# Query, key and value loads one pair earlier, and the shared chunk's tanh ahead of a pair's exponentials

## The chip, the cores and the metric

The kernel runs on one core of one Trainium2 chip. The metric is the device time of one execution, in microseconds (us).

## The reference, cut to what matters

```python
def _attn_ref(q, k, v, cap):                       # q, k, v: 2 x 12 x 448 x 64
    scores = (1.0 / np.sqrt(64)) * np.matmul(q, k.transpose(0, 1, 3, 2))
    scores = cap * np.tanh(scores / cap)
    scores = scores - np.max(scores, axis=-1, keepdims=True)
    attn = np.exp(scores)
    attn = attn / (np.sum(attn, axis=-1, keepdims=True) + 1e-09)
    return np.matmul(attn, v).astype(np.float32)
...
    x = np.ascontiguousarray(attn_out.transpose(0, 2, 1, 3)).reshape(B * S, H * D)   # 896 x 768
    x = _moe_ref(x=x, **moe_kwargs)      # x @ w_in, h * sigmoid(1.702 h), @ w_out
    return _moe2_ref(x=x, **moe2_kwargs) # rms norm, silu(x @ w_gate) * (x @ w_val), @ w_out
```

Everything is float32.

## The kernel before, in words

The program has two parts. `attention()` (lines 193 to 508) works on 12 pairs of heads (`NPR`); `rest()` (line 510 on) does the two feed-forward layers, with TensorE as its main engine. A scheduler does not reorder anything: every engine and every DMA queue runs its instructions in the order in which the Python code issues them. All loads and stores named here go to SyncE's queue (SPq in the profile).

A pair's k and q arrive as float32 in a tile `kq` and are split by VectorE into a high and a low part (`split_kq`, a cast in line 253 and a subtraction in line 254), so that three products give the accuracy. A head's 448 keys are three chunks of 128 and a rest of 64; the two heads' rests share a fourth chunk, the shared chunk (`NC`).

The loop of line 442 has 13 passes. Pass p, for 0 < p < 12, issues per engine:

- SyncE: `load_kq(p + 2)` (lines 217, 218: k 256 KB, q 224 KB), `load_v(p + 1)` (line 224, 256 KB), in the first three passes a weight tile `raw` (line 112, 768 KB), `spread(p - 3)` (line 367, which reads back the reciprocals of an earlier pair from DRAM), and late in the pass `keep_recips(p - 1)` (line 362, which stores the reciprocals of pair p-1 to DRAM and so waits for line 357).
- TensorE: score products of chunks 1 and 2 of pair p and chunk 0 of pair p+1 (`scores`, line 272, six products each), the shared chunk's (`scores_last`, line 280, three), the outputs of pair p-1 (`outputs`, line 318, 32 products), the sums of its exponentials (`sums`, line 352, 16).
- ScalarE: tanh of the three chunks (line 299), the exponential of chunks 0 and 1 (`exp(pa[p])`, line 302), a decode step if `plan_a` has one, the shared chunk's tanh (`tanh(p, NC)`, line 299), the exponential of the rest (`exp(pb[p])`).
- VectorE: `norm(p - 5)` from pass 5 on (lines 386, 398, 405), `split_kq(p + 2)`, `add_two(p)` (line 336, adds the two halves of `pa`), decode steps if `plan_d` has any, `copy_out(p - 1)` (line 330), the reciprocal of the sums of pair p-1 (line 357).
- GpSimd: `add_third(p)` (line 340, adds a part of `pb` to the tile of `add_two`).

The decode steps unpack the first weight tiles, whose words hold floats: on ScalarE `size` (line 127), `high_part` (line 174); on VectorE `clip` (131), `field` (135), `top` (159), `low` (165), `low_part` (179). In passes 1 to 6 `plan_a` and `plan_d` (lines 427 to 434) put them between the others; `clip` of a tile needs its `size`, `low_part` its `high_part`.

Buffers make further waits. `kq` has two, `v` three. The pool `ps_v` has two PSUM buffers, taken in turn by `scores_last(p)`, `outputs(p - 1)`, `sums(p - 1)`, `scores_last(p + 1)` and so on: `scores_last(p + 1)` waits for `copy_out(p - 1)`, `outputs(p)` for the reciprocal of pair p-1, `sums(p - 1)` for `tanh(p, NC)`. Of the scores' three buffers, each is free again after its tanh.

Of the kernel before, what the change touches and what calls it, by code (L numbers as in the profile page):

```python
# [8 lines left out]
F32 = mybir.dt.float32  # L9
# [8 lines left out]
def attn_moe_kernel(  # L18
# [15 lines left out]
    B, D = 2, 64  # L34
# [8 lines left out]
    NC = 3  # L43
# [63 lines left out]
    def load_to(u):  # L107
        while nload[0] <= min(u, len(units) - 1):
            w = nload[0]
            t = pools['raw'].tile([128, 6, 128, 2], U32, tag="raw", name="raw")  # L110
            for b0, n, s in units[w]:
                nc.sync.dma_start(out=t[:, b0:b0 + n].rearrange("p k f t -> p k (f t)"), in_=s)
            raw_t[w] = t
            nload[0] += 1
# [66 lines left out]
    def run(op, w):  # L181
        if w < len(units) and (op, w) not in done:
            done.add((op, w))
            op(w)
# [8 lines left out]
    def attention():  # L193
        with ExitStack() as actx:
            ap_ = actx.enter_context(tc.tile_pool(name="at", bufs=2, reuse_waits="tile"))
# [5 lines left out]
            XW = KW + S  # L201
# [9 lines left out]
            xs, raws, vs, pa, pb, zt, nr, ts_ = {}, {}, {}, {}, {}, {}, {}, {}  # L211

            def load_kq(p):
                if p >= NPR:
                    return
                t = raws[p] = ap_.tile([128, XW], F32, tag="kq", name="kq")
                nc.sync.dma_start(out=t[:, 0:KW], in_=k[p])
                nc.sync.dma_start(out=t[:, KW:XW], in_=q[p])

            def load_v(p):  # L220
                if p >= NPR:
                    return
                vs[p] = ap_.tile([128, 2 * (NC + 1), D], F32, tag="v", name="v", bufs=3)
                nc.sync.dma_start(out=vs[p].rearrange("p c d -> p (c d)"), in_=v[p])

            cuts = [slice(KW, XW), slice(0, 128), slice(128, KW)]
# [22 lines left out]
            def split_kq(p):  # L249
                t = raws.pop(p)  # L250
                x = ap_.tile([128, 2, XW], F32R, tag="x", name="x", bufs=3)
                xs[p] = [(x[:, a, KW:XW], (x[:, a, 0:KW],)) for a in range(2)]
                nc.vector.tensor_copy(x[:, 0], t)  # L253
                nc.vector.tensor_tensor(out=x[:, 1], in0=t, in1=f(x[:, 0]), op=ALU.subtract)
# [11 lines left out]
            def scores(p, c):  # L266
                if p >= NPR:
                    return
                ps = sc[p, c] = ps_s.tile([128, 2, 512], F32, tag="s", name="s")
                for n, (a, m) in enumerate(TERMS):  # L270
                    for e in range(2):
                        nc.tensor.matmul(
                            out=ps[:, e, 0:S], lhsT=keys(p, a, c)[half[e]],
                            rhs=xs[p][m][0][half[e]], start=(n == 0), stop=(n == 2),
                        )

            def scores_last(p):
                ps = sc[p, NC] = ps_v.tile([128, 512], F32, tag="v", name="v")
                for n, (a, m) in enumerate(TERMS):
                    nc.tensor.matmul(  # L280
                        out=ps[:, 0:S], lhsT=keys(p, a, NC), rhs=xs[p][m][0], start=(n == 0), stop=(n == 2)
                    )

            def tanh(p, c):
                if p >= NPR:
                    return
                if c == 0:
                    pa[p] = ap_.tile([128, 2, 2, S], F32, tag="pa", name="pa", bufs=3)
                if c == 2:
                    pb[p] = ap_.tile([128, 3, S], F32, tag="pb", name="pb", bufs=3)  # L290
                if c < 2:
                    t = pa[p][:, c]
                elif c == 2:
                    t = pb[p][:, 0:2]
                else:
                    t = pb[p][:, 2]
                src_ = sc.pop((p, c))
                src_ = src_[:, 0:S] if c == NC else src_[:, :, 0:S]
                nc.scalar.activation(out=t, in_=src_, func=AF.Tanh, scale=tsc)  # L299

            def exp(t):
                nc.scalar.activation(out=t, in_=t, func=AF.Exp, scale=capt)  # L302
# [7 lines left out]
            def outputs(p, cs=range(NC + 1)):  # L310
                if 0 in cs:
                    opened[p] = ps_v.tile([128, 512], F32, tag="v", name="v")
                ps = opened[p]
                for c in cs:
                    for n in range(4):
                        e, d0 = n // 2, n % 2 * 32
                        w = vs[p][:, e * NC + c if c < NC else 2 * NC + e]
                        nc.tensor.matmul(  # L318
                            out=ps[32 * n:32 * n + 32, 0:S], lhsT=w[:, d0:d0 + 32],
                            rhs=probs(p, c)[:, e] if c < NC else pb[p][:, 2],  # L320
                            start=(c == 0), stop=(c == NC), skip_group_check=True,
                        )
# [41 lines left out]
            def spread(p):  # L364
                d = nr[p].rearrange("(e j) n -> e (j n)", j=2)
                nr[p] = zrp.tile([128, S], F32, tag="r", name="r", bufs=3)
                nc.sync.dma_start(out=nr[p], in_=d.unsqueeze(1).to_broadcast([2, 64, S]))
# [41 lines left out]
            def norm(p):  # L409
                for step in (norm_mul, norm_hi, norm_lo):  # L410
                    step(p)
# [7 lines left out]
            constants()  # L419
            load_kq(1)  # L420
            load_v(0)

            warm = ps_v.tile([128, 512], F32, tag="v", name="v")
            for _ in range(WARM):
                nc.tensor.matmul(out=warm[:, 0:S], lhsT=ones, rhs=xA[0][:, 0, 0:S], start=True, stop=True)

            plan_a = {
                1: [(size, 0)], 2: [(size, 1)], 3: [(high_part, 0)], 5: [(high_part, 1)],
                12: [(square, 2), (sign, 2), (mask, 2)],
            }  # L430
# [5 lines left out]
            def decode(plan, p):  # L436
                for op in plan.get(p, ()):
                    run(*op)

            split_first(ts, x)  # L440

            for p in range(NPR + 1):
                load_kq(p + 2)
                load_v(p + 1)
                if p < 3:
                    load_to(p)
                if p == 0:
                    scores(0, 0)
                    tanh(0, 0)
                    exp(pa[0][:, 0])  # L450
                    scores(0, 1)
                    tanh(0, 1)
                    exp(pa[0][:, 1])
                    scores(0, 2)
                    tanh(0, 2)
                    scores_last(0)
                    tanh(0, NC)
                    exp(pb[0])
                    outputs(0, (0,))
                    split_kq(1)  # L460
                    scores(1, 0)
                    outputs(0, (1,))
                elif p < NPR:
                    tanh(p, 0)
                    scores(p, 1)
                    tanh(p, 1)
                    scores(p, 2)
                    tanh(p, 2)
                    exp(pa[p])
                    decode(plan_a, p)  # L470
                    scores(p + 1, 0)
                    scores_last(p)
                    tanh(p, NC)
                    exp(pb[p])
                else:
                    decode(plan_a, p)
                if 3 <= p < NPR:
                    spread(p - 3)
                if 5 <= p < NPR - 2:
                    norm(p - 5)  # L480
                if p + 2 < NPR:
                    split_kq(p + 2)
                if p < NPR:
                    add_two(p)
                decode(plan_d, p)
                if p == 1:
                    outputs(0, (2, NC))
                elif p:
                    outputs(p - 1)
                if NPR - 1 <= p:  # L490
                    spread_late(p - 2)
                if p:
                    if p < NPR:
                        copy_out(p - 1, "D")
                    sums(p - 1)
                    if p < NPR - 2:
                        keep_recips(p - 1)
                if p < NPR:
                    add_third(p)
                if NPR - 3 <= p < NPR:  # L500
                    norm(p - 4)
                if p == NPR:
                    copy_out(p - 1, "A")
                    some = (p - 3, p - 2, p - 4)
                    for step in (norm_mul, norm_hi, norm_lo):
                        for q_ in some:
                            step(q_)
# [340 lines left out]
    with tc.manual_schedule():  # L848
        tail = attention()
        rest(*tail)  # L850
# [64 lines left out]
```

## Time and profile before

| | |
|---|---|
| Runs | 623.2, 625.25, 626.21 us; median 625.25 us |
| Profiled execution | 623.85 us, its span 622.1 us |
| TensorE (PE) busy | 591.3 us, 95% of the span, mean granted clock 0.988 |
| VectorE (DVE) busy | 454.4 us, 73% |
| ScalarE (ACT) busy | 389.4 us, 63% |
| GpSimd (POOL) busy | 65.8 us, 11% |
| DMA | 67.91 MB, mean 109 GB/s |

A line of a timeline gives the start, the duration, the engine and line, the operation with the tile that it writes and the one it reads, a count, and in brackets how long the engine was idle before it and what ended that. PE is TensorE's products, PEld its weight loads. PEclk is the granted share of TensorE's full clock of 2.4 GHz, so 0.50 is 1.2 GHz. The duration shown reaches to where the result has left the engine; the next instruction may start a little sooner.

### The profile page before, as it was taken

How to read it: one execution, taken by the hardware profiler on the slowest of the kernel's cores; microseconds unless marked ns; L12 is line 12 of the kernel's file. 1: busy time of each engine (PE TensorE's matmuls, PEld its weight loads, DVE VectorE, ACT ScalarE, POOL GpSimd, SP SyncE). 2: the span in 40 equal slices, each digit the busy share in tenths (PEclk: the TensorE clock that was granted, in tenths of full speed). 3: DMA queues.
4: the chain of work that ended last, by engine and by line, in shares of the span. 5: the costliest groups of instructions: out<-in, count | busy, mean ns of one | idle time of the engine just before them, and what ended most of it. 6: DMA issues, size and time to landing. Idle time of an engine off the chain costs nothing.

```text
span 622.1 us, 8470 instructions
## 1 busy us (share of the span) xinstructions
PE 591.3 (95%) x3385; PEld 499.4 (80%) x3385; DVE 454.4 (73%) x553; ACT 389.4 (63%) x507; POOL 65.8 (11%) x51
## 2 busy tenths in 40 slices
PE   7857887899999999999999999999999999999997
PEld 4423333389989888888988989999988899999997
DVE  5676678779866644666778899998388887688842
ACT  6956668679975554777866774766456674356400
POOL 0221222100000000000012201210022200022100
PEclk9987999999999999999999999999999999999999
DMA  8332532116335241333333332334123343332012
GB/s 277 102 115 72 163 122 84 44 53 200 119 129 155 83 125 55 122 128 103 103 102 101 106 126 91 136 102 153 52 101 103 102 152 104 100 103 102 0 72 106
DMA packets 54449, 67.91 MB, mean 109 GB/s; under 512 B 2918, under 2 KB 49162, under 8 KB 54410
## 3 DMA queue, kind: packets, MB, share of 16 engines
q1 hardware_dynamic: 54122, 67.15, 33.4%
q8 instruction: 26, 0.43, 0.3%
q10 hardware_dynamic: 288, 0.23, 0.1%
q14 instruction: 13, 0.11, 0.1%
HBM read 64.59 MB, written 2.78 MB: 108 GB/s over the span
## 4 chain that ended last, share of the span: by engine, by line
PE 82%; DVE 8%; DMA 4%; ACT 2%; issue 2%; SPq 1%; DVEq 0%
PE b L568 22%; PE b L567 22%; PE b L566 22%; PE b L776 14%; DMA kq<-in_q 4%; DVE rs L357 2%; DVE ts L336 2%; PE v L318 2%; DVE x L253 1%; DVE z L330 1%; DMA first<-in_k 1%; ACT pa L302 1%; ACT pa L299 1%; DVE dec L159 1%; DVE dec L165 1%
## 5 line engine op out<-in xcount | busy, mean ns | idle before, releaser
L566 PE MATMUL b<-x,ring 128*128 128x512 f32 (+1 forms) x480 | 174.0, 362 | 2.2 <-DVE z L389 2.2
L568 PE MATMUL b<-x,ring 128*128 128x512 f32 (+1 forms) x480 | 174.3, 363 | 0.0
L567 PE MATMUL b<-x,ring 128*128 128x512 f32 (+1 forms) x480 | 174.1, 363 | 0.0
L566 PEld LDWEIGHTS b<-x,ring 128*128 128x128 f32 x480 | 90.1, 188 | 12.7 <-DVE z L389 2.6
L567 PEld LDWEIGHTS b<-x,ring 128*128 128x128 f32 x480 | 90.1, 188 | 9.9
L568 PEld LDWEIGHTS b<-x,ring 128*128 128x128 f32 x480 | 90.1, 188 | 9.4
L776 PE MATMUL b<-ring,uA 128*128 128x384 f32 x504 | 87.8, 334 | 0.0
L776 PEld LDWEIGHTS b<-ring,uA 128*128 128x128 f32 x504 | 87.4, 188 | 0.0
L153 DVE SCALAR_TENSOR_TENSOR dec<-raw,dec 128x768 uint32<-128x768 uint32 x66 | 67.8, 1028 | 24.7 <-ACT dec L149 23.4
L159 DVE SCALAR_TENSOR_TENSOR dec<-raw,dec 128x768 uint32<-128x768 uint32 x68 | 75.1, 1104 | 1.1
L179 DVE TENSOR_TENSOR ring<-dec,ring 128x768 fp32r<-128x768 f32 x68 | 66.8, 984 | 4.5 <-ACT ring L174 4.5
L568 PE MATMUL b<-g,ring 128*128 128x384 f32 (+1 forms) x192 | 70.0, 365 | 0.0
L567 PE MATMUL b<-g,ring 128*128 128x384 f32 (+1 forms) x192 | 69.9, 364 | 0.0
L566 PE MATMUL b<-g,ring 128*128 128x384 f32 (+1 forms) x192 | 69.6, 362 | 0.0
L165 DVE SCALAR_TENSOR_TENSOR dec<-raw,dec 128x768 uint32<-128x768 uint32 x68 | 66.7, 981 | 1.5
L174 ACT ACTIVATE ring<-dec 128x768 fp32r<-128x768 f32 x68 | 56.7, 834 | 17.4 <-DVE dec L165 8.7
L145 ACT ACTIVATE dec<-dec,edge 128x768 f32<-128x768 f32 x66 | 61.5, 932 | 1.0
L141 ACT ACTIVATE dec<-raw 128x768 f32<-128x768 f32 x66 | 59.1, 896 | 0.5 <-DVE ring L179 0.5
L149 ACT ACTIVATE dec<-dec 128x768 f32<-128x768 f32 x66 | 55.6, 843 | 1.5
L744 POOL TENSOR_TENSOR a<-a,gg 128x512 f32<-128x512 f32 (+1 forms) x18 | 29.3, 1628 | 188.9 <-DVE gg L737 188.9
L747 ACT ACTIVATE uA<-a 128x512 fp32r<-128x512 f32 (+1 forms) x24 | 13.9, 578 | 46.3 <-POOL a L744 34.5
L598 DVE TENSOR_TENSOR g<-gg,g 128x384 fp32r<-128x384 f32 (+1 forms) x32 | 20.0, 626 | 27.4 <-ACT g L595 27.2
(92 smaller groups left out, 648.2 us busy)
## 6 DMA issues: line engine op xcount, KB each, us to landing
raw<-in_moe_w_out SPq DMA_DIRECT2D x20, 768.0 KB
raw<-in_moe_w_in SPq DMA_DIRECT2D x16, 768.0 KB
raw<-in_moe_w_gate SPq DMA_DIRECT2D x12, 768.0 KB
raw<-in_moe_w_val SPq DMA_DIRECT2D x12, 768.0 KB
raw<-in_moe_w_out SPq DMA_DIRECT2D x8, 512.0 KB
v<-in_v SPq DMA_DIRECT2D x12, 256.0 KB
kq<-in_k SPq DMA_DIRECT2D x11, 256.0 KB
kq<-in_q SPq DMA_DIRECT2D x11, 224.0 KB
```

Source lines behind the costliest of these rows:

```text
L141: nc.scalar.activation(out=f(d), in_=f(hi), func=AF.Square, scale=2.0 ** 15)
L145: nc.scalar.activation(out=f(d), in_=f(d), func=AF.Sign, bias=edge)
L149: nc.scalar.activation(out=f(d), in_=f(d), func=AF.Relu, scale=2.0 - 2.0 ** -23)
L153: nc.vector.scalar_tensor_tensor(out=d, in0=hi, scalar=3, in1=d, op0=ALU.logical_shift_left, op1=ALU.bitwise_and)
L159: nc.vector.scalar_tensor_tensor(out=d, in0=hi, scalar=0xC0000000, in1=d, op0=ALU.bitwise_and, op1=ALU.bitwise_or)
L165: nc.vector.scalar_tensor_tensor(out=d, in0=lo, scalar=29, in1=d, op0=ALU.logical_shift_right, op1=ALU.bitwise_or)
L174: nc.scalar.activation(out=t[:, 0], in_=f(dec_t[w][0]), func=AF.Copy)
L179: nc.vector.tensor_tensor(out=t[:, 1], in0=f(d), in1=f(t[:, 0]), op=ALU.subtract)
L566: nc.tensor.matmul(out=wide(o, b), lhsT=w0, rhs=x0, start=first, stop=False)
L567: nc.tensor.matmul(out=wide(o, b), lhsT=w0, rhs=x1, start=False, stop=False)
L568: nc.tensor.matmul(out=wide(o, b), lhsT=w1, rhs=x0, start=False, stop=last)
L776: nc.tensor.matmul(out=os_[t][n][:, 0:HW], lhsT=uA[xi][:, i, tok], rhs=w[:, wi, n * HW:(n + 1) * HW], start=(i == 0 and xi == 0 and wi == ...
```

## The change

Pass p loads k and q of pair p+3 instead of p+2, into three buffers instead of two, and v of pair p+2 instead of p+1, into four instead of three; ahead of the loop one more pair's k, q and v are loaded. On ScalarE the shared chunk's tanh moves ahead of `exp(pa[p])`, so that both exponentials follow it, and the decode step of `plan_a` moves behind both. TensorE's order stays the same, and so does VectorE's.

```diff
--- before.py
+++ after.py
@@ -213,14 +213,14 @@
             def load_kq(p):
                 if p >= NPR:
                     return
-                t = raws[p] = ap_.tile([128, XW], F32, tag="kq", name="kq")
+                t = raws[p] = ap_.tile([128, XW], F32, tag="kq", name="kq", bufs=3)
                 nc.sync.dma_start(out=t[:, 0:KW], in_=k[p])
                 nc.sync.dma_start(out=t[:, KW:XW], in_=q[p])
 
             def load_v(p):
                 if p >= NPR:
                     return
-                vs[p] = ap_.tile([128, 2 * (NC + 1), D], F32, tag="v", name="v", bufs=3)
+                vs[p] = ap_.tile([128, 2 * (NC + 1), D], F32, tag="v", name="v", bufs=4)
                 nc.sync.dma_start(out=vs[p].rearrange("p c d -> p (c d)"), in_=v[p])
 
             cuts = [slice(KW, XW), slice(0, 128), slice(128, KW)]
@@ -419,6 +419,8 @@
             constants()
             load_kq(1)
             load_v(0)
+            load_kq(2)
+            load_v(1)
 
             warm = ps_v.tile([128, 512], F32, tag="v", name="v")
             for _ in range(WARM):
@@ -440,8 +442,8 @@
             split_first(ts, x)
 
             for p in range(NPR + 1):
-                load_kq(p + 2)
-                load_v(p + 1)
+                load_kq(p + 3)
+                load_v(p + 2)
                 if p < 3:
                     load_to(p)
                 if p == 0:
@@ -466,12 +468,12 @@
                     tanh(p, 1)
                     scores(p, 2)
                     tanh(p, 2)
-                    exp(pa[p])
-                    decode(plan_a, p)
                     scores(p + 1, 0)
                     scores_last(p)
                     tanh(p, NC)
+                    exp(pa[p])
                     exp(pb[p])
+                    decode(plan_a, p)
                 else:
                     decode(plan_a, p)
                 if 3 <= p < NPR:
```

## Rows read from the trace of the kernel before

**Rows 1.** Windows: us, busy time of PE, PEld, DVE, ACT, POOL, granted clock, DMA share, GB/s.

```profile
24.00:70.00 46.00, 33.54 (x276) 15.42 (x268) 31.57 (x30) 29.45 (x28) 10.13 (x4) 0.85 0.38 118
70.00:106.00 36.00, 28.52 (x276) 13.90 (x276) 26.59 (x34) 26.39 (x26) 8.55 (x5) 1.00 0.39 130
...
124.00:622.00 498.00, 494.59 (x2532) 452.65 (x2530) 367.12 (x449) 303.07 (x424) 41.04 (x28) 1.00 0.33 106
```

**Rows 2.** Timeline, VectorE's reciprocals, first and eleventh: start us, us, engine, line, operation.

```profile
20.97 1.55 DVE L357 RECIPROCAL rs<-v 128x224 f32<-128x224 f32 x1
...
117.06 1.56 DVE L357 RECIPROCAL rs<-v 128x224 f32<-128x224 f32 x1 [0.69 <-PE v L352]
```

**Rows 3.** Chain of waits in order of time, one period: start us, us, what.

```profile
95.91 1.48 DVE rs L357
97.40 0.50 SPq L362
...
98.43 2.80 DMA kq<-in_q
101.33 0.67 DVE x L253
...
103.09 1.08 DVE ts L336
104.18 0.54 DVE z L330
104.72 1.48 DVE rs L357
```

**Rows 4.** Waits, 0 to 135 us: us in total, times, longest.

```profile
DVE x L253 <- DMA kq<-in_q: 24.8, 9, 4.4
```

**Rows 5.** Timeline, VectorE's norm steps, first and last of three.

```profile
59.67 0.55 DVE L386 TENSOR_TENSOR z<-z,r 128x448 f32<-128x448 f32 x1
...
60.69 0.63 DVE L405 TENSOR_TENSOR x<-z,x 128x448 fp32r<-128x448 f32 x1
```

**Rows 6.** Timeline, TensorE in the pass without a following pair.

```profile
106.23 1.71 PE L318 MATMUL v<-pa,v 128*32 128x448 f32 x16 [0.59 <-DVE rs L357]
...
110.14 1.49 PE L272 MATMUL s<-x 64*128 64x448 f32 x12
...
112.35 1.71 PE L318 MATMUL v<-pa,v 128*32 128x448 f32 x16
```

**Rows 7.** Timeline, TensorE's scores_last after two gaps; in brackets the gap.

```profile
33.67 1.49 PE L280 MATMUL v<-x 128*128 128x448 f32 x3 [3.58 <-DVE z L330]
...
78.41 0.86 PE L280 MATMUL v<-x 128*128 128x448 f32 x3 [1.73 <-DVE z L330]
```

**Rows 8.** Timeline, ScalarE: exp(pa), shared tanh, exp(pb).

```profile
104.04 1.79 ACT L302 ACTIVATE pa<-pa,capt 128x1792 f32<-128x1792 f32 x1
...
105.72 0.63 ACT L299 ACTIVATE pb<-v,tsc 128x448 f32<-128x448 f32 x1
...
106.38 1.42 ACT L302 ACTIVATE pb<-pb,capt 128x1344 f32<-128x1344 f32 x1
```

**Rows 9.** Timeline, GpSimd's addition and decode steps with and without it.

```profile
19.96 0.56 DVE L135 TENSOR_SCALAR dec<-dec 128x768 uint32<-128x768 uint32 x1
...
29.37 0.95 DVE L159 SCALAR_TENSOR_TENSOR dec<-raw,dec 128x768 uint32<-128x768 uint32 x1
...
30.35 2.72 DVE L165 SCALAR_TENSOR_TENSOR dec<-raw,dec 128x768 uint32<-128x768 uint32 x1
...
42.48 2.24 POOL L340 TENSOR_TENSOR ts<-ts,pb 128x896 f32<-128x896 f32 x1 [10.22 <-DVE ts L336]
...
42.81 2.32 DVE L135 TENSOR_SCALAR dec<-dec 128x768 uint32<-128x768 uint32 x1
```

**Rows 10.** Timeline, ScalarE in pass 1: last tanh of three, size step.

```profile
15.65 1.00 ACT L299 ACTIVATE pb<-s,tsc 128x896 f32<-128x896 f32 x1
...
18.22 0.90 ACT L127 ACTIVATE dec<-raw 128x768 f32<-128x768 f32 x1
```

## The prediction

> **What bounds the kernel now.** I read the windows first. From 124 us to the end TensorE is busy 494.6 of 498 us, so that part can lose nothing by earlier loads; the change is confined to the attention loop before it, where TensorE has idle time and in 24 to 70 us a mean granted clock of only 0.85 [rows 1]. Whatever the loop saves moves the rest forward one for one, since no row behind it hangs on a clock time.
>
> I call the loop's pass p "pass p" and count periods by VectorE's reciprocals (line 357), because SyncE, TensorE and VectorE all hand over there. The first starts at 20.97, the eleventh at 117.06: ten periods take 96.1 us [rows 2].
>
> Next the chain of waits, over one period of 8.81 us [rows 3]. It runs: reciprocal 1.48, then SyncE issues the store of the reciprocals at 97.40 and only behind it the next pair's k and q, the q at 98.43; the transfer takes 2.80; cast and subtraction run from 101.33 to 103.09; add_two to 104.18; copy_out 0.54; and the next reciprocal. The load's own buffer is long free: what holds the load back is that it stands in SyncE's queue behind a store that waits for the reciprocal, and the split of its data is nearly the next thing VectorE does. The waits say the same: VectorE waits nine times for kq, 24.8 us in all, about 2.8 each [rows 4].
>
> **The loads.** After the change pass p issues the load of pair p+3, which VectorE splits in pass p+1. It still stands behind the store of pass p-1, but it has a whole period to land, and it needs about 3.9 us (97.40 to 101.33 [rows 3]). The buffer it takes, of pair p, was split in pass p-2; v's fourth buffer was last read by the outputs of pass p-1, before the reciprocal that releases the store. So no new wait on SyncE. The front has one more k, q and v (736 KB) ahead of the first weight tile: bounded by one more landing, 2.80, while the first reader of that tile itself comes 2.2 later (below); I take nothing, at most 0.6. With the load gone from the chain, what is late next is worked out per queue:
>
> - VectorE's own work without decoding: reciprocal 1.48, the three norm steps 1.65 (59.67 to 60.69 plus 0.63 [rows 5]), cast and subtraction 1.76, add_two 1.09, copy 0.54: 6.5.
> - TensorE: from one output block to the next in the only pass without a following pair 6.12, plus the missing six score products, half of 1.49: 6.86 [rows 6].
> - ScalarE: exp(pa) to the start of exp(pb) 2.34 with the shared tanh between, exp(pb) 1.42 [rows 8], three tanhs of at most 1.00 each [rows 10]: at most 6.8, not above TensorE.
>
> **ScalarE's order.** It stays the same work, but it makes a loop. exp(pa) now stands behind the shared chunk's tanh; that needs scores_last, which needs the PSUM buffer that copy_out of two passes back frees; and copy_out stands on VectorE behind add_two, which needs exp(pa). Round that loop: copy 0.54, scores_last 0.86 [rows 7], tanh 0.66, exp(pa) 1.79 [rows 8], add_two 1.09 and four hand-overs of 0.05 (an estimate): 5.1. Plus whatever decoding stands between add_two and copy_out. In passes 2 to 4 that is two operations, and with the new order exp(pb) ends a little after add_two, so GpSimd's add_third starts behind the first of the two and holds up the second: the field step took 2.32 beside the addition of 2.24 and 0.56 without it; the low step 2.72, where its like, line 159, took 0.95 undisturbed [rows 9]. So 0.95 + 2.24 + 0.95 = 4.1 in passes 2 and 4, and 0.56 + 2.24 + 0.56 = 3.4 in pass 3, where clip is priced as its neighbour of the same size. If the second operation never lost its turn, 2.24 would be saved three times; both ends go into the range, and I take the blocked price, because the two blocked rows are these same instructions.
>
> The Trainium skill ("SBUF — State Buffer", Who interferes with whom) says that VectorE and GpSimd share a port pair as a lock and that the one that starts first makes the other wait out the whole instruction. By it add_third beats the second decode step in all three passes and the sum below stands; were it sharing instead of locking, the time would be up to 6.7 lower. The pair of rows for the field step agrees with it.
>
> Pass 1 pays once more. The first weight tile's size step moves from behind exp(pa) (18.22) to behind exp(pb): tanh(2) ends at 16.65 [rows 10], + 0.66 + 1.68 (start to start) + 1.42 = 20.4 [rows 8], + 0.90 = 21.3. VectorE's clip needs it, and by then add_third has begun: 20.45 + 2.24 = 22.7, then clip 0.56, field 0.56, copy 0.54: the first reciprocal at 24.4 instead of 20.97.
>
> **The sum.** First reciprocal 24.4. Pass 2: 5.1 + 4.1 = 9.2. Pass 3: 8.5. Pass 4: 9.2. Pass 5, VectorE's queue with one decode step (norm has begun): 6.5 + 0.95 = 7.4. Pass 6 the same, 7.4. Passes 7 to 10 lie between VectorE's 6.5 and TensorE's 6.86; TensorE is first a little ahead, I take 6.6 each, 26.4. Pass 11 has no following pair, 6.12, and exp(pa) 0.4 later: 6.5. Total 24.4 + 9.2 + 8.5 + 9.2 + 7.4 + 7.4 + 26.4 + 6.5 = 99.0, against 117.06: 18.1 less. The same laying-out of the old order, with the load in the chain, gives 95.3 for the ten periods against the 96.1 measured, so I trust it to about 1 us, more for what it has not seen. The clock helps: TensorE's gaps of 3.6 us came ahead of products that took 1.49 instead of 0.86, while after a gap of 1.73 they took 0.86 [rows 7]; in the new layout I find no gap over 2 us.
>
> The profiled execution took 623.85 (span 622.1), so 605.7; the median of the runs is 625.25, 1.4 higher, so about 607.
>
> **Rivals.**
> 1. *The new ScalarE order costs nothing* (scores_last is ready before its turn, decoding fits beside). Then passes 2 to 4 fall to between 6.5 and 8 and the first reciprocal stays near 21: some 7 us less, 600. For it: TensorE has room in these passes. Against: the old rows show scores_last waiting for copy_out even with exp(pa) ahead of it (3.58 [rows 7]).
> 2. *TensorE stays at the lower clock in the decoding passes.* In 24 to 70 us the mean was 0.85, so about 2 x 0.15 x 46 = 13.8 us at the half clock [rows 1]. The new loop has less slack there; the same 13.8 us would do 6.9 us less work: 614. Against: in 70 to 106 us TensorE was busy 28.5 of 36 us, 79%, at full clock [rows 1], and the new passes are as full (6.86 of 8.5 to 9.2).
> 3. *The loads don't come earlier in effect, and it ends slower.* If landing takes more than the 6.5 us that VectorE needs for a period, because each transfer now queues behind v and a weight tile, the split waits as before and only the ScalarE order is left: 3.4 later in pass 1, nothing regained: 625.25 + 3.4 = 628.7. It decides from that one number, issue to landing over about 6 us; the old rows have 2.80.
>
> **How the numbers follow.** Forecast 0.64, rival 1 0.18, rival 2 0.12, rival 3 0.06. The range 599 to 615 takes in the forecast with its bounds and rivals 1 and 2; it leaves out rival 3 and some tails. A change of 0.5% (3.1 us), about what a measurement of this kernel can tell from none, is reached by all but rival 3: faster 0.93, within 0.5% 0.03 (a mild rival 3 or a heavy rival 2), slower 0.04.
>
> **What would show it.** Right: VectorE's wait at line 253 for kq gone or under 2 us; reciprocals about 6.5 to 7 apart from pass 7 on and 8 to 9 in passes 2 to 4, the first near 24; the line for the shared tanh ahead of exp(pa) with ScalarE idle before it in passes 2 to 4, released by scores_last, itself released by copy_out; granted clock 1.0 nearly throughout; from the first wide product on nothing changed. Wrong: periods still above 8.5 in passes 7 to 10 (loads, rival 3), a low clock in 25 to 65 us (rival 2), or passes 2 to 4 under 7.5 (rival 1).

## The result and the profile after

The changed kernel takes 604.55 us in the median of four runs (604.28 to 606.27), the kernel before 624.91 (four runs). The ratio is 0.9682, 95% interval 0.9651 to 0.9712: 20 us faster. The forecast was 607.0, with a range of 599 to 615. The profiled execution took 604.75, its span 603.0 against 622.1.

The windows of the kernel after, with the columns of [rows 1]:

```profile
24.00:70.00 46.00, 41.25 (x406) 20.52 (x407) 44.52 (x48) 38.83 (x38) 13.22 (x6) 0.96 0.54 169
70.00:87.00 17.00, 17.00 (x173) 8.98 (x173) 16.00 (x20) 16.27 (x16) 6.00 (x3) 1.00 0.31 101
...
104.00:603.00 499.00, 495.50 (x2529) 453.54 (x2527) 366.42 (x447) 302.47 (x423) 41.05 (x28) 1.00 0.32 106
```

In 24 to 70 us TensorE is now busy 41.3 of 46 us, where it was busy 33.5, and VectorE 44.5 instead of 31.6. The feed-forward part, from 104 us on, is filled as before, 495.5 of 499 us; what became of its length is told under the clock below.

VectorE's reciprocals in the timeline of the kernel after, the first six and the eleventh, which answer to [rows 2]:

```profile
23.60 1.55 DVE L357 RECIPROCAL rs<-v 128x224 f32<-128x224 f32 x1
...
32.19 1.54 DVE L357 RECIPROCAL rs<-v 128x224 f32<-128x224 f32 x1
...
40.49 1.54 DVE L357 RECIPROCAL rs<-v 128x224 f32<-128x224 f32 x1
...
49.17 1.54 DVE L357 RECIPROCAL rs<-v 128x224 f32<-128x224 f32 x1
...
56.37 1.55 DVE L357 RECIPROCAL rs<-v 128x224 f32<-128x224 f32 x1
...
63.56 1.55 DVE L357 RECIPROCAL rs<-v 128x224 f32<-128x224 f32 x1
...
96.21 1.56 DVE L357 RECIPROCAL rs<-v 128x224 f32<-128x224 f32 x1 [0.19 <-PE v L352]
```

The first comes 2.6 later than before, at 23.60 instead of 20.97; the eleventh 20.9 earlier, at 96.21 instead of 117.06. So the ten periods shrank from 96.1 to 72.6 us, the second to fourth pass (8.59, 8.30, 8.68) staying the longest.

Three lines of the waits of the kernel after, 0 to 120 us, in total, times, longest; the last answers to [rows 4]:

```profile
ACT pb L299 <- PE v L280: 3.5, 3, 1.4
...
PE v L280 <- DVE z L330: 3.2, 3, 1.2
...
DVE x L253 <- DMA kq<-in_q: 0.6, 1, 0.6
```

VectorE's 24.8 us of waiting for k and q have become 0.6. The wait that the prediction named is there but short: ScalarE waits for scores_last three times, in passes 2, 4 and 5, 3.5 us in all, and TensorE ahead of it for copy_out, 3.2. The kernel before had both waits too, 5.4 and 15.7 in 0 to 135 us; what is new is that exp(pa) now stands behind them.

The chain of waits in order of time, from pass 3 to pass 4 of the kernel after, start and duration:

```profile
34.30 1.69 ACT pa L302
...
36.08 1.09 DVE ts L336
37.17 0.48 DVE dec L131
...
37.68 1.25 DVE dec L135
38.93 1.03 issue
39.96 0.62 DVE z L330
...
40.63 0.89 PE v L280 x3
...
41.54 0.63 ACT pb L299
```

No transfer is left in it. It is the loop that the prediction laid out, in its order: exp(pa) at 34.30, add_two, clip and field, copy_out at 39.96, scores_last at 40.63, the shared tanh at 41.54 and behind that the next exp(pa). What fills it beyond the plain steps is the decoding: 37.17 to 39.96, of which two undisturbed steps would take 1.1. The timeline shows why, here in passes 2 and 3:

```profile
26.99 1.09 DVE L336 TENSOR_TENSOR ts<-pa 128x896 f32<-128x896 f32 x1
...
28.00 0.95 DVE L159 SCALAR_TENSOR_TENSOR dec<-raw,dec 128x768 uint32<-128x768 uint32 x1
...
28.34 2.57 POOL L340 TENSOR_TENSOR ts<-ts,pb 128x896 f32<-128x896 f32 x1 [6.21 <-ACT pb L302]
...
28.99 2.74 DVE L165 SCALAR_TENSOR_TENSOR dec<-raw,dec 128x768 uint32<-128x768 uint32 x1
...
31.65 0.61 DVE L330 COPY z<-v 128x448 f32<-128x448 f32 x1
...
37.36 2.27 POOL L340 TENSOR_TENSOR ts<-ts,pb 128x896 f32<-128x896 f32 x1 [6.44 <-ACT pb L302]
37.68 2.36 DVE L135 TENSOR_SCALAR dec<-dec 128x768 uint32<-128x768 uint32 x1
```

The first decode step runs 0.95, GpSimd's addition is ready meanwhile and goes next, and the second decode step, which takes 0.96 alone (experiment 1), stands 2.74. The lines of pass 3, the last two, repeat it with the field step, 2.36. They answer to [rows 9].

### The profile page after: what moved, and what is told of

The parts are those of the page before. It is cut to its first block, busy times and chain, and to the rows that moved or that the text cites. A ratio compares the mean times of both kernels' runs of the same rounds, so it can differ in the third digit from the quotient of the medians.

```text
span 603.0 us, 8469 instructions
## 1 busy us (share of the span) xinstructions
PE 586.1 (97%) x3385; PEld 500.2 (83%) x3385; DVE 455.1 (75%) x553; ACT 388.7 (64%) x507; POOL 65.9 (11%) x51
## 4 chain that ended last, share of the span: by engine, by line
PE 90%; DVE 5%; ACT 3%; issue 1%; DMA 1%; SPq 0%; DVEq 0%
PE b L570 23%; PE b L569 23%; PE b L568 23%; PE b L778 14%; PE v L318 4%; PE s L272 2%; DVE rs L357 1%; ACT pa L302 1%; PE v L352 1%; PE v L280 1%; ACT pb L299 1%; DMA first<-in_k 1%; ACT pa L299 1%; DVE ts L336 1%; DVE z L330 0%
```

## The experiments

Each run was timed in rounds with the kernel before on the same chip, so times are compared by their ratios to it. "Loads" stands for the change's loads with their buffers, "order" for its ScalarE order.

**1. The loads alone.** The change without this part of it:

```diff
-                    exp(pa[p])
-                    decode(plan_a, p)
                     scores(p + 1, 0)
                     scores_last(p)
                     tanh(p, NC)
+                    exp(pa[p])
                     exp(pb[p])
+                    decode(plan_a, p)
```

> The change's loads and buffers with ScalarE's old order (exp(pa), decode step, shared tanh, exp(pb)). Theory (the loads bring the gain, the new ScalarE order costs some 7 us of it): the eleventh reciprocal starts near 90 instead of 96.2, the time is about 598, a ratio to the kernel before of about 0.957; the first reciprocal is back near 21 and passes 2 to 4 take 8.2, 6.4 and 8.1. Rival (the new order costs nothing or helps): the same as with the whole change, 604.5 or more, ratio 0.968 or more.

597.55 us, ratio 0.9567 (0.9549 to 0.9586): 7 us faster than the whole change. Lines of its timeline:

```profile
20.73 1.55 DVE L357 RECIPROCAL rs<-v 128x224 f32<-128x224 f32 x1
...
27.26 0.96 DVE L165 SCALAR_TENSOR_TENSOR dec<-raw,dec 128x768 uint32<-128x768 uint32 x1
...
28.12 2.12 POOL L340 TENSOR_TENSOR ts<-ts,pb 128x896 f32<-128x896 f32 x1 [5.00 <-ACT pb L302]
...
35.12 1.55 DVE L357 RECIPROCAL rs<-v 128x224 f32<-128x224 f32 x1
...
89.95 1.56 DVE L357 RECIPROCAL rs<-v 128x224 f32<-128x224 f32 x1 [0.71 <-PE v L352]
```

The first reciprocal is back at 20.73. In pass 2 the low step (line 165) starts before GpSimd's addition and takes 0.96. The loads carry more than the whole gain, and the new order gives some of it back.

**2. The order alone**, the same lines put into the kernel before.

> The new ScalarE order with the old loads. Theory: the load chain still sets the period; only pass 1 is late, the first reciprocal near 24 instead of 21, so 2 to 4 us slower than before, about 628, ratio 1.004 to 1.006. Rival (the new order carries part of the gain): faster than before, ratio under 0.99.

627.47 us, ratio 1.0046 (1.0031 to 1.0061), 0.5% slower, as expected. Its waits:

```profile
DVE x L253 <- DMA kq<-in_q: 25.0, 9, 4.5
...
ACT pb L299 <- PE v L280: 20.7, 9, 4.4
```

The wait for the load stays at 25.0 us, and ScalarE waits 20.7 us for scores_last, nine times. In the kernel before scores_last came about as late (TensorE waited 15.7 us there for copy_out, 14.8 here), but ScalarE had exp(pa) to do meanwhile and waited 5.4. The new order costs only 3 us here, and all of it in pass 1: the first reciprocal is at 23.89 instead of 20.97, the eleventh at 119.96, and the ten periods between take 96.1 us as before. That fits with the load chain being longer than the loop round the tanh.

**3. The buffers alone.**

```diff
-                t = raws[p] = ap_.tile([128, XW], F32, tag="kq", name="kq")
+                t = raws[p] = ap_.tile([128, XW], F32, tag="kq", name="kq", bufs=3)
...
-                vs[p] = ap_.tile([128, 2 * (NC + 1), D], F32, tag="v", name="v", bufs=3)
+                vs[p] = ap_.tile([128, 2 * (NC + 1), D], F32, tag="v", name="v", bufs=4)
```

> Three buffers for k and q and four for v, everything else as before: loads are still issued two pairs and one pair ahead. Theory (the load waits in SyncE's queue behind the store of the reciprocals, not for a buffer): no change, ratio 0.998 to 1.002, VectorE's wait for kq still about 25 us in all. Rival (a buffer holds the load back): most of the 20 us of the change, ratio about 0.97.

624.78 us, ratio 1.0003 (0.9986 to 1.002): no change, and the wait for k and q is where it was:

```profile
DVE x L253 <- DMA kq<-in_q: 26.2, 8, 4.5
```

**4. The distance of k and q alone**, in the old two buffers, v and ScalarE as before:

```diff
             load_kq(1)
             load_v(0)
+            load_kq(2)
...
-                load_kq(p + 2)
+                load_kq(p + 3)
                 load_v(p + 1)
```

> Only k and q are loaded three pairs ahead, in the old two buffers; v stays one pair ahead in three buffers and ScalarE keeps its old order. Theory (what counts is that the load of a pair is issued one turn earlier in SyncE's queue): all of the gain of the loads, 597 to 598.5, ratio 0.955 to 0.959. Rival (the extra buffers, or v two pairs ahead, carry a part): slower than the run of the loads alone by more than 1.5 us, ratio over 0.960.

597.16 us, ratio 0.9558 (0.953 to 0.9587), the same as experiment 1 within the intervals. Its wait for the loads:

```profile
DVE x L253 <- DMA kq<-in_q: 0.2, 1, 0.2
```

Experiments 3 and 4 are a pair: buffers without an earlier issue bring nothing, an earlier issue without buffers brings everything. Neither the extra k and q buffer nor the v part is needed for this gain.

**5. The decode step between the exponentials**, the rest of the change as it is:

```diff
                     exp(pa[p])
-                    exp(pb[p])
                     decode(plan_a, p)
+                    exp(pb[p])
```

> The whole change, but with ScalarE's decode step between the two exponentials instead of behind both; the shared tanh stays ahead. Theory: pass 1's share of the new order's cost goes, the first reciprocal near 21.7 instead of 23.6 and the loop round the shared tanh stays; 2 to 4 us faster than the whole change, about 601, ratio about 0.962. Rival (the place of the tanh is all of the cost, not the decode step): no difference from the whole change, 0.968.

601.24 us, ratio 0.962 (0.9604 to 0.9636), against 0.9682 some 4 us faster than the whole change (0.0062 x 624.9 = 3.9). The first, third and fourth reciprocal in its timeline:

```profile
21.70 1.55 DVE L357 RECIPROCAL rs<-v 128x224 f32<-128x224 f32 x1
...
35.98 1.55 DVE L357 RECIPROCAL rs<-v 128x224 f32<-128x224 f32 x1
...
45.65 1.54 DVE L357 RECIPROCAL rs<-v 128x224 f32<-128x224 f32 x1
```

The first is at 21.70, as expected, 1.9 earlier than with the whole change, half of the gain. Passes 2 and 3 gain too (14.28 from 21.70 to 35.98, against 16.89), since the step in between delays exp(pb) and with it GpSimd. They are as short as in experiment 1 (14.39, from 20.73 to 35.12), which has the tanh in its old place: in these two passes the tanh ahead of exp(pa) costs nothing by itself. Pass 4 has no ScalarE step between the exponentials and is the longest here, 9.67 us.

**6. The addition moved off GpSimd in passes 2 to 4**, otherwise the whole change:

```diff
-                eng = nc.gpsimd if 0 < p < NPR - 1 else nc.vector
+                eng = nc.gpsimd if p == 1 or 4 < p < NPR - 1 else nc.vector
```

> The whole change, but in passes 2 to 4 VectorE does add_third itself, after its reciprocal, instead of GpSimd. Theory (GpSimd's addition makes the second decode step wait inside the loop round the shared tanh): the decode steps at line 165 and 135 fall from 2.7 and 2.4 to about 1.0 and 0.6, periods 2 to 4 fall from 8.6, 8.3 and 8.7 to about 7.7, 7.2 and 7.7, together some 2.5 to 3 us faster than the whole change: 601.5 to 602, ratio 0.963 to 0.964. Rival (the waiting was hidden): VectorE only gets 3 us more work and the time is 604.5 to 607.5.

602.73 us, ratio 0.9637 (0.9608 to 0.9667). The interval still overlaps that of the whole change (0.9651 to 0.9712), so the reading rests on the trace. The timeline in passes 2 and 3:

```profile
27.80 0.95 DVE L159 SCALAR_TENSOR_TENSOR dec<-raw,dec 128x768 uint32<-128x768 uint32 x1
...
28.78 0.96 DVE L165 SCALAR_TENSOR_TENSOR dec<-raw,dec 128x768 uint32<-128x768 uint32 x1
...
32.20 1.03 DVE L340 TENSOR_TENSOR ts<-ts,pb 128x896 f32<-128x896 f32 x1
...
37.55 0.56 DVE L135 TENSOR_SCALAR dec<-dec 128x768 uint32<-128x768 uint32 x1
```

The second decode steps are down to 0.96 and 0.56, and periods 2 to 4 take 22.8 us (23.40 to 46.20) instead of 25.6 (23.60 to 49.17): 2.8 less, although VectorE does three more additions of 1.03. One of these falls into pass 5, which has the norm steps as well and takes 8.19 instead of 7.20. In the end 1.9 us are left at the eleventh reciprocal, 94.28 instead of 96.21. So the waiting behind GpSimd was on the path.

**7. The tanh back between the exponentials, the decode step still behind both:**

```diff
+                    exp(pa[p])
                     scores(p + 1, 0)
                     scores_last(p)
                     tanh(p, NC)
-                    exp(pa[p])
                     exp(pb[p])
                     decode(plan_a, p)
```

> The change's loads; the shared tanh back between the two exponentials, but the decode step still behind both. Theory (what costs is that the size step is late in pass 1 and that exp(pb) ends so soon after exp(pa) that GpSimd's addition gets in ahead of the second decode step; with only the tanh of 0.66 between them it still does): the first reciprocal near 23.5, periods 2 to 4 about 0.4 shorter each than with the whole change, 603 to 603.8, ratio 0.965 to 0.967. Rival (the shared tanh's place ahead of exp(pa) carries half of the cost, through its wait for scores_last): 600.5 to 601.5, ratio about 0.961 to 0.9625.

601.57 us, ratio 0.9618 (0.9593 to 0.9644): the rival's number, and my forecast of it missed by at least 1.4 us. The timeline of passes 2 to 4 tells which mechanism it was:

```profile
28.31 2.65 POOL L340 TENSOR_TENSOR ts<-ts,pb 128x896 f32<-128x896 f32 x1 [5.88 <-DVE ts L336]
...
29.04 2.73 DVE L165 SCALAR_TENSOR_TENSOR dec<-raw,dec 128x768 uint32<-128x768 uint32 x1
...
36.99 0.56 DVE L135 TENSOR_SCALAR dec<-dec 128x768 uint32<-128x768 uint32 x1
...
37.32 2.20 POOL L340 TENSOR_TENSOR ts<-ts,pb 128x896 f32<-128x896 f32 x1 [6.36 <-ACT pb L302]
...
44.33 0.95 DVE L159 SCALAR_TENSOR_TENSOR dec<-raw,dec 128x768 uint32<-128x768 uint32 x1
```

In pass 2 the second decode step still loses, 2.73. In pass 3 it starts at 36.99, 0.3 ahead of GpSimd, and takes 0.56; in pass 4 it wins as well, 0.95 (44.33, the addition at 44.40). I had expected 0.66 of tanh between the exponentials to be too little for that. So the time came back, but through the order of VectorE and GpSimd. ScalarE's wait for scores_last is gone in this run too; whether it cost anything beside the order of the two engines, the run doesn't separate. In passes 2 and 3 of experiment 5 the tanh's place cost nothing.

**8. Products in TensorE's gap ahead of the feed-forward part**, on top of experiment 1:

```diff
+    FILL = 9
...
                 if p == NPR:
                     copy_out(p - 1, "A")
+                    fill = ps_s.tile([128, 2, 512], F32, tag="s", name="fill")
+                    for _ in range(FILL):
+                        nc.tensor.matmul(
+                            out=fill[:, 0, 0:S], lhsT=ones, rhs=xA[0][:, 0, 0:S], start=True, stop=True
+                        )
```

> The change's loads with ScalarE's old order, and nine products into an unused PSUM tile between the last sums of attention and the first feed-forward product, where TensorE has been idle for 2.16 us in each run. Theory (the granted clock falls to 0.50 for some 3.4 us behind that gap in some executions, which costs about 1.7 us): no fall behind the gap, 595.5 to 597, ratio 0.953 to 0.9555. Rival (the gap isn't what the clock answers to, or the products delay the first one): clock and time as without them, 597.5 or more.

596.63 us, ratio 0.9545 (0.9525 to 0.9565), the fastest of all, though its interval overlaps that of experiment 1 (0.9549 to 0.9586). The gap is closed to 0.15 us:

```profile
94.15 2.07 PE L509 MATMUL fill<-x,ones 128*128 128x448 f32 x9
...
96.38 0.44 PE L574 MATMUL b<-x,ring 128*128 128x384 f32 x1 [0.15 <-DVE z L390]
```

All five executions had a mean granted clock of 0.999 or 1.000 and lie between 596.48 and 597.22; of the four of experiment 1 two had 0.996 and 0.997 and took 598.85 and 598.12, the other two 596.45 and 596.98. Experiment 4, without the products too, had one such in four (0.997, 598.35). So the products don't make the best execution better, they seem to make the slower ones rare; with five executions against eight that is likely, not settled.

## Why the prediction was right

**The loads** were right step by step: the wait for k and q went from 24.8 to 0.6 us, no transfer is left on the chain, and no wait of SyncE for a buffer or a store has taken its place there. SyncE's one new long wait, 4.4 us for a store to land before it is read back (line 367), comes behind the last load of k, q and v. One short wait is new on VectorE, of the norm for the reciprocals that come back from DRAM (r), 0.23 and 0.32 us in the timeline:

```profile
78.31 0.62 DVE L386 TENSOR_TENSOR z<-z,r 128x448 f32<-128x448 f32 x1 [0.23 <-DMA r<-recs]
...
85.12 0.62 DVE L386 TENSOR_TENSOR z<-z,r 128x448 f32<-128x448 f32 x1 [0.32 <-DMA r<-recs]
```

That no buffer held the load back is shown by experiments 3 and 4. That it stood in SyncE's queue behind the store was read off the chain [rows 3]; it fits experiment 4, where one turn earlier was enough, and all eight stores of the kernel before that a load of k and q follows, where the load is issued 0.55 to 0.68 us behind the store's start. The direct trial, the same load ahead of the store in the same pass, was not made.

**The periods.** Forecast 9.2, 8.5 and 9.2 in passes 2 to 4; measured 8.59, 8.30, 8.68. Passes 5 and 6: 7.4 against 7.20 and 7.19. Passes 7 to 10: 26.4 against 25.9 (63.56 to 89.43). Pass 11: 6.5 against 6.78. In all the eleventh reciprocal was summed to 99.0 and came at 96.21; the prediction trusted its sum to about 1 us, and it was off by 2.8: 0.8 in pass 1, 1.3 in passes 2 to 4, 0.9 in passes 5 to 10, and 0.3 the other way in pass 11.

In passes 2 to 4 one term was mis-sized, the blocked second decode step. The sum added GpSimd's addition and behind it the whole step, 2.24 + 0.95 and 2.24 + 0.56. But the rows that it cites show the two together: the blocked steps of 2.72 and 2.32 [rows 9] have the waiting in them. From the first decode step to copy_out it was 3.65 in pass 2 (28.00 to 31.65) and 3.66 in pass 4 (44.97 to 48.63) instead of 4.1, and 2.87 in pass 3 (37.09 to 39.96) instead of 3.4: 1.4 in all. Another error is smaller: the sum added durations as shown, which reach to the result, where the next instruction on the same engine starts earlier. exp(pa) counted 1.79 and holds the chain for 1.69; add_two counted 1.09, and the decode step behind it starts 1.01 after it (26.99 to 28.00). That is 0.1 to 0.2 a pass, about what passes 5 and 6 came out short.

**Pass 1.** Forecast 24.4, measured 23.60. The mechanism was the one named. In the timeline of the kernel after, ScalarE's size step, GpSimd's addition and the clip:

```profile
19.82 0.87 ACT L127 ACTIVATE dec<-raw 128x768 f32<-128x768 f32 x1
20.05 2.09 POOL L340 TENSOR_TENSOR ts<-ts,pb 128x896 f32<-128x896 f32 x1 [17.85 <-ACT pb L302]
...
20.72 1.83 DVE L131 TENSOR_SCALAR dec<-dec 128x768 f32<-128x768 f32 x1 [0.99 <-ACT dec L127]
```

The clip waited for GpSimd as priced, and stands 1.83 with the waiting. The sum had the addition end at 22.7; it ended at 22.14, because it began 0.4 sooner, nearly all of that from the pass itself (its third tanh starts at 15.30 instead of 15.65 [rows 10]), and took 2.09 instead of 2.24.

**ScalarE's order** was priced at some 7 us, the distance to rival 1. The difference between experiment 1 and the whole change is 0.0115 of 624.9, 7.2 us. Of the profiles' 6.3 us at the eleventh reciprocal (89.95 and 96.21) 2.9 are there at the first one already (20.73 and 23.60) and the other 3.4 come in passes 2 to 4. Rival 1 was thus wrong: the new order costs about what the prediction charged for it.

**GpSimd and VectorE.** Experiments 6 and 7 agree with what the Trainium skill says in "SBUF — State Buffer" (Who interferes with whom): the order of starting decides, and the loser waits out the whole instruction. The same decode step took 0.56 when it started 0.3 ahead of the addition, and 2.36 behind it in pass 3 of the changed kernel.

**The clock.** Here the prediction was partly wrong. Right was that the clock rises in the loop: the mean of 24 to 70 us went from 0.85 to 0.96. But the prediction found no gap over 2 us in the new layout and expected nothing to change from the first feed-forward product on. It overlooked TensorE's gap of 2.16 us just ahead of that product, which the kernel before has too. From the eleventh reciprocal to the end of the span took 505.0 us before (622.1 - 117.06) and 506.8 after. Two stretches of the kernel after, and one of the kernel before:

```profile
25.00:30.00 5.00, 4.80 (x36) 1.47 (x40) 4.79 (x6) 5.00 (x5) 1.66 (x1) 0.66 0.57 155
103.00:113.00 10.00, 10.00 (x50) 9.14 (x51) 5.39 (x11) 5.22 (x8) 0.00 (x0) 0.83 0.00 0
```

```profile
124.00:134.00 10.00, 10.00 (x59) 8.83 (x58) 6.68 (x12) 6.75 (x11) 0.00 (x0) 1.00 0.00 0
```

After two gaps of 1.57 and 1.23 us in pass 1 the granted clock in 25 to 30 us was 0.66, part of it at 1.2 GHz; that delayed the outputs of pass 2, and with them the next scores_last, to 32.74. But that waited for VectorE's copy_out anyway, which was late too and ended at 32.26, so about half a microsecond of the delay counted. And in the first products of the feed-forward part it was 0.83 where the kernel before had 1.00: 10 x 0.17 = 1.7 us, about the 1.75 missing. The other profiles agree: from the eleventh reciprocal to the end took 504.95 to 505.14 us in the four in which the clock stayed at 1.00 there, and 506.35 to 506.79 in the six in which it fell.

So the lower clock that rival 2 feared held for only about three us in the passes that it named, and came again in a place that it didn't name, where it took back 1.75 of the 2.8 us that the sum had overpriced. What was left of these two errors of opposite sign is the 1.0 us between the sum, 605.7, and the profiled execution, 604.75; that it is so little is luck. The forecast of 607 lies another 1.4 higher, by the step from the profiled execution to the median, which in the kernel after is 0.2 the other way.

**Rival 3**, loads that land too late, is excluded by the waits.

## What to carry to other kernels

Ask of a late transfer what stands before it in its queue, not only which buffer it needs: here one turn earlier in the code was worth 28 us and the buffers nothing. An engine that gets its input sooner can get in ahead of a more urgent one: when two engines exclude each other, look at who will now start first. And try the parts of a change one by one, since a gain of 20 us hid a loss of 7.

## What the runs showed of the hardware that was not expected

TensorE stood idle for 2.16 us ahead of the first feed-forward product in nine of the ten kernels profiled, each time between the same two groups of products, attention's last sums and the first feed-forward product. In six profiles (the changed kernel, experiments 1, 3, 5, 6 and 7) the granted clock then fell to 0.50 for about three us; in three (the kernel before, experiments 2 and 4) it stayed at 1.00. Neither the length of the gap nor the version decides it; what does is open. Nor does one gap's length tell elsewhere: 1.73 us left the clock at full in the kernel before [rows 7] and 1.59 in pass 1 of experiment 5, while in pass 1 of the changed kernel it fell behind 1.57 and 1.23, and in that of experiment 7 behind 0.75 and 1.24.
